# Attention and GEGLU on one core: unit transposes by DMA with the product on GpSimd, GELU bursts over two batches, and a planner that knows the port shared by VectorE and GpSimd

## The chip, the core and the metric

The kernel runs on one core of one Trainium2 chip. The engines are named as the profile names them: PE (TensorE, matrix products), ACT (ScalarE, here the softmax exp and GELU), DVE (VectorE), POOL (GpSimd), SP (the queue that issues DMAs). The kernel divides PSUM, into which PE writes, into eight banks of 128 x 512 fp32. Time runs some 2 us longer than the profiled span of the same run.

## The reference

One transformer block, 2048 tokens wide 640: 32 query heads of 20 that share one key and value head, then a GEGLU feed-forward layer of 1536.

```python
h  = x + attention(layernorm(x), wq, wk, wv, wo)
h2 = h + feed_forward(layernorm(h), w_gate, w_up, w_down)
# attention: scores = q k^T * 20**-0.5; p = softmax(scores); (p v) wo, no mask
# feed_forward: (gelu(x w_gate) * (x w_up)) w_down, tanh form of GELU
```

## The kernel before

The program is written by a small list scheduler that runs when the kernel is built. It keeps a clock for each engine, takes the engine that is free first, and commits the best ready operation with a cost in ns. The engines then run these lists in order, with semaphores. A wrong cost is no error in the result; it yields an order in which an engine later waits.

The work on scores is what fills the time. There are 512 packs of four score tiles (128 keys x 512 columns). PE computes a pack into four banks. Each tile goes either to ACT (a true exp) or to DVE (an exp made of one multiply-add whose integer result is read as bf16). A DVE tile needs two shifted copies as well, made by adding a constant ("shift-add"), mostly on POOL, and costs three products with v where an ACT tile costs one. The scheduler chooses 0, 1 or 2 tiles of a pack for DVE by how busy DVE is; while ACT is in a GELU burst it may give DVE all four.

Sixteen packs make a unit (32 units, two or four of them a "chunk" of tokens). A unit's sum leaves PSUM as `osb`, is transposed and divided by the softmax sum:

```python
def on_job(u, so):                      # before: transpose on PE by identity
    for j in range(4):
        pieces.append((mm(..., osb[:, so, j*P:(j+1)*P], ident[:], True, True), ...))
    # then, from PSUM: DVE reciprocal of the sums, and DVE products into onq (two per unit)
```

When all units of a chunk are done, wo, the second layernorm and the feed-forward layer of that "batch" (nine batches, 0 to 8) run under the exps of later chunks. The gate products are copied to `gbuf` by DVE; when a batch's are complete, ACT runs GELU over them in one burst and goes back to exp. After the last exp what is left runs as a tail, and there GELU is applied from PSUM directly.

```python
if gate_left[b] == 0:                   # before: one burst per batch
    gelu(b)                             # then: up products, then down products
```

When PE has been busy less than half of the last 3.4 us, the scheduler adds products with zeros ("fills").

The softmax here doesn't subtract the row's maximum and nothing guards it: scores larger than these inputs give would overflow.

## Time and profile before

804.31 us median of 3 runs (803.94 to 805.19). The profiled run was a further one of 806.45 us.

| engine | busy us | share of the 804.6 us span |
|---|---|---|
| ACT | 750.6 | 93% |
| PE | 693.7 | 86% |
| DVE | 627.2 | 78% |
| POOL | 586.2 | 73% |

The groups of instructions of the kernel before, shapes kept apart: engine, operation, output and inputs, shapes, count, busy us and mean ns of one, idle time before them and what ended it.

```profile
L1486 POOL TENSOR_TENSOR pd<-pd,shifts 128x512 int32<-128x512 int32 x517 | 534.8, 1043 | 170.5 <-DVE pd L1509 161.1 <-PE ps L510 4.8 <-DVE ln_veb L419 1.4
L1423 ACT ACTIVATE pa<-ps 128x1024 bf16<-128x1024 f32 x449 | 484.7, 1082 | 2.4 <-PE ps L1083 2.3
L1509 DVE TENSOR_SCALAR pd<-ps 128x512 uint16<-128x512 f32 x587 | 395.3, 687 | 142.3 <-PE ps L1083 131.3
L1423 ACT ACTIVATE pa<-ps 128x512 bf16<-128x512 f32 x563 | 354.9, 653 | 23.8 <-PE ps L1083 19.2
...
L472 DVE TENSOR_SCALAR xn_tmp<-xh,mv,ln_r 128x640 bf16<-128x640 bf16 x32 | 21.4, 686 | 0.4
L1466 DVE TENSOR_SCALAR pd<-pd 128x512 uint16<-128x512 uint16 x43 | 21.4, 502 | 0.0
...
L668 DVE TENSOR_TENSOR onq<-ps,rcp 128x160 bf16<-128x160 f32 x56 | 16.0, 317 | 0.7
...
L829 ACT ACT_TABLE_LOAD x7 | 9.0, 1283 | 0.1
L1423 ACT ACT_TABLE_LOAD x7 | 9.0, 1283 | 0.0
```

ACT ran 449 x 2 + 563 = 1461 exp tiles, DVE 587. The mean shift-add of 512 columns on DVE took 502 ns (276 at best) and the mean normalisation 686 (422 at best). Seven GELU bursts of one batch cost 7 + 7 table loads, and an eighth load to GELU follows in the tail.

Busy us of each engine in stretches of time, before; the columns after POOL are PE's granted clock, the share of the DMA engines and GB/s.

```profile
core 0: us, PE busy (x) PEld busy (x) DVE busy (x) ACT busy (x) POOL busy (x), PEclk, DMA share, GB/s
100.00:200.00 100.00, 85.77 (x1572) 38.98 (x1572) 81.42 (x145) 97.10 (x140) 77.37 (x81) 0.97 0.04 9
600.00:700.00 100.00, 90.59 (x1962) 44.43 (x1958) 77.81 (x137) 98.28 (x138) 76.07 (x76) 0.98 0.06 13
160.00:165.00 5.00, 1.68 (x24) 0.51 (x21) 4.98 (x9) 4.97 (x5) 3.34 (x4) 0.85 0.00 0
165.00:170.00 5.00, 4.75 (x60) 1.60 (x52) 1.88 (x5) 4.31 (x7) 0.95 (x1) 0.50 0.01 2
```

In the long stretches ACT is busy 97 to 98%: attention is bound by ACT.

The timeline of ACT before, near the end: start, length, instruction, count, idle time before it.

```profile
728.50 1.28 ACT L829 ACT_TABLE_LOAD   x1
729.79 2.86 ACT L829 ACTIVATE gbuf<-gbuf 128x1536 bf16<-128x1536 bf16 x2
732.66 1.28 ACT L1423 ACT_TABLE_LOAD   x1
733.95 2.49 ACT L1423 ACTIVATE pa<-ps 128x512 bf16<-128x512 f32 x4
...
770.51 8.34 ACT L1423 ACTIVATE pa<-ps 128x512 bf16<-128x512 f32 x12 [0.17 <-PE ps L1083]
778.87 1.28 ACT L811 ACT_TABLE_LOAD   x1
```

The burst is 1.28 + 2.86 + 1.28 us, back to back. The last exp ends at 770.51 + 8.34 = 778.9 us, so the tail is 804.6 - 778.9 = 25.7 us.

### The profile page before, as it was taken

The page shows a single profiled execution, that of the slowest core. Times are in us where ns is not written, and L with a number is a line of the kernel's source. Part 1 is how long each engine was busy: PE and PEld are TensorE (multiplying, and loading weights), DVE is VectorE, ACT ScalarE, POOL GpSimd, SP SyncE. Part 2 cuts the span into 40 slices and gives each one's busy share as a digit, 9 for nine tenths or more (in the row PEclk, how much of TensorE's full clock was granted, in tenths as well). Part 3 has the DMA queues.
Part 4 walks back from the last instruction along what each step waited for, and adds up shares of the span by engine and source line. Part 5 has one row for each costly group of instructions (what it writes and reads, how often), then busy time and mean ns, then how long its engine had stood idle before and what let it go on. Part 6 is the DMA issues. An engine that isn't in the chain of part 4 may idle for free.

```text
span 804.6 us, 29858 instructions
## 1 busy us (share of the span) xinstructions
PE 693.7 (86%) x13162; PEld 332.3 (41%) x13162; DVE 627.2 (78%) x1156; ACT 750.6 (93%) x1065; POOL 586.2 (73%) x624
## 2 busy tenths in 40 slices
PE   5687778989978998789988799888998899887998
PEld 3332223534434443345433444334444444343457
DVE  7868789877887778877788777988779776877864
ACT  5899999999989999899999999999999999999981
POOL 4587877868767677767878678877777668776760
PEclk9999999989999999999999999999999999998999
DMA  7680001000100000000000000000010000100000
GB/s 198 118 311 2 2 13 24 3 2 2 35 19 3 2 20 18 18 3 3 19 19 18 3 2 19 19 19 2 2 35 19 3 2 19 19 18 11 11 19 18
DMA packets 40288, 21.96 MB, mean 27 GB/s; under 512 B 31328, under 2 KB 38880, under 8 KB 40160
## 3 DMA queue, kind: packets, MB, share of 16 engines
q1 hardware_dynamic: 38848, 19.61, 9.6%
q8 instruction: 105, 1.72, 0.9%
q10 hardware_dynamic: 1312, 0.44, 0.3%
q14 instruction: 23, 0.19, 0.1%
HBM read 10.21 MB, written 2.62 MB: 16 GB/s over the span
## 4 chain that ended last, share of the span: by engine, by line
PE 46%; DVE 25%; ACT 25%; issue 2%; DMA 1%; POOL 1%; POOLq 0%; DVEq 0%
ACT pa L1423 25%; PE ps L510 17%; DVE pd L1509 15%; PE ps L1083 13%; PE ps L1162 13%; DVE pd L1466 3%; PE ps L506 3%; DVE xn_tmp L472 2%; DVE osb L1189 1%; DVE stats L403 1%; DVE qT L580 1%; DVE xh L728 1%; DVE onq L668 1%; DMA onT<-onq 1%; DVE ln_vb L415 0%
## 5 line engine op out<-in xcount | busy, mean ns | idle before, releaser
L1423 ACT ACTIVATE pa<-ps 128x512 bf16<-128x512 f32 (+1 forms) x1012 | 699.4, 844 | 26.2 <-PE ps L1083 21.5
L1486 POOL TENSOR_TENSOR pd<-pd,shifts 128x512 int32<-128x512 int32 x517 | 534.8, 1043 | 170.5 <-DVE pd L1509 161.1
L1509 DVE TENSOR_SCALAR pd<-ps 128x512 uint16<-128x512 f32 x587 | 395.3, 687 | 142.3 <-PE ps L1083 131.3
L1162 PE MATMUL ps<-pd,v_ext 128*32 128x512 bf16 x1761 | 276.2, 400 | 28.0 <-DVE osb L1189 21.5
L1162 PE MATMUL ps<-pa,v_ext 128*32 128x512 bf16 x1461 | 265.4, 393 | 2.7 <-ACT pa L1423 1.3
L1083 PE MATMUL ps<-qT,kT 32*128 32x512 bf16 x2048 | 206.8, 390 | 65.9 <-DVE pd L1509 41.0
L1083 PEld LDWEIGHTS ps<-qT,kT 32*128 32x128 bf16 x2048 | 58.9, 91 | 233.7 <-DVE pd L1509 161.3
L1162 PEld LDWEIGHTS ps<-pd,v_ext 128*32 128x32 bf16 x1761 | 74.8, 98 | 79.1 <-issue 35.0
L1162 PEld LDWEIGHTS ps<-pa,v_ext 128*32 128x32 bf16 x1461 | 70.6, 96 | 43.1 <-issue 30.3
L510 PE MATMUL ps<-xn2T,wg_sb 128*32 128x256 bf16 (+1 forms) x1720 | 66.1, 278 | 0.1
L510 PE MATMUL ps<-xn2T,wu_sb 128*32 128x256 bf16 x1680 | 64.9, 276 | 0.5 <-DVE onq L668 0.4
L510 PE MATMUL ps<-wd_sb,gbuf 128*32 128x320 bf16 x1344 | 64.4, 301 | 0.2 <-DVE onq L668 0.2
L510 PE MATMUL ps<-xn1T,wq_pad 128*32 128x256 bf16 (+1 forms) x1440 | 51.0, 267 | 0.2
L510 PEld LDWEIGHTS ps<-xn2T,wu_sb 128*32 128x32 bf16 x1680 | 42.9, 97 | 18.7 <-issue 10.3
L510 PEld LDWEIGHTS ps<-xn2T,wg_sb 128*32 128x32 bf16 x1720 | 42.1, 98 | 17.6 <-issue 11.5
L510 PEld LDWEIGHTS ps<-wd_sb,gbuf 128*32 128x32 bf16 x1344 | 33.5, 96 | 23.8 <-issue 11.8
L510 PEld LDWEIGHTS ps<-xn1T,wq_pad 128*32 128x32 bf16 x1440 | 33.8, 98 | 13.8 <-issue 8.9
L846 DVE TENSOR_TENSOR gbuf<-ps,gbuf 128x512 bf16<-128x512 f32 x48 | 32.9, 685 | 6.6 <-PE ps L506 6.4
L1466 DVE TENSOR_SCALAR pd<-pd 128x512 uint16<-128x512 uint16 (+2 forms) x66 | 37.8, 595 | 0.0
L1472 POOL TENSOR_TENSOR pd<-pd,shifts 128x256 int32<-128x256 int32 x48 | 30.2, 635 | 3.9 <-DVE pd L1509 3.4
L403 DVE BATCH_NORM_STATS2 stats<-xh 128x6 f32<-128x320 bf16 x64 | 29.9, 477 | 1.3 <-DMA xh<-in_A_x_dram 1.1
L809 DVE CAST gbuf<-ps 128x512 bf16<-128x512 f32 x42 | 28.7, 683 | 1.0 <-PE ps L510 0.9
(71 smaller groups left out, 357.8 us busy)
## 6 DMA issues: line engine op xcount, KB each, us to landing
out_dram<-xh SPq DMA_DIRECT2D x16, 160.0 KB, 1.8
xh<-in_A_x_dram SPq DMA_DIRECT2D x3, 640.0 KB, 6.3
wg_sb<-in_B_w_gate_dram SPq DMA_DIRECT2D x1, 1920.0 KB, 9.3
wu_sb<-in_B_w_up_dram SPq DMA_DIRECT2D x1, 1920.0 KB, 13.6
wd_sb<-in_B_w_down_dram SPq DMA_DIRECT2D x1, 1920.0 KB, 18.0
wo_sb<-in_A_wo_dram SPq DMA_DIRECT2D x1, 800.0 KB, 5.5
gbuf<-in_A_wq_dram ACTq DMA_DIRECT2D x1, 400.0 KB, 4.6
gbuf<-in_A_wq_dram SPq DMA_DIRECT2D x1, 400.0 KB, 6.9
```

What stands on the lines that cost most here:

```text
L403: dve(lambda e: e.bn_stats(stats[:, ln, t, 6 * h:6 * h + 6], xh[:, t, h * HALF:(h + 1) * HALF]), 395, [key], [("st", ln, t, h)], prio, c)
L506: return e.matmul(o(b), l, r, start=st, stop=sp)
L510: ins = e.matmul(o(b)[a, :], l[:, a], r, start=st, stop=sp, tile_position=(0, 32 * j))
L809: dve(lambda e: e.tensor_copy(o, i), c_dve(n * k), [("b", bk)], ks, 1.0, fin)
L846: dve(lambda e: e.tensor_tensor(o, i, o, ALU.mult), c_dve(n * k), [("b", bk)] + ks, ks, 1.0, fin)
L1083: ins = e.matmul(bank(b), kT4[32 * r:32 * r + 32, kt * P:(kt + 1) * P], qT[32 * r:32 * r + 32, s, :], start=True, stop=True, tile_position ...
L1162: ins = e.matmul(ps[32 * r:32 * r + 32, ab * 512:(ab + 1) * 512], v_ext[:, it["kt"], it["w"], :], it["ap"], start=st, stop=(j in ends), ti ...
L1423: op = plan.commit("act", lambda e: e.activation(dst, src, ACT.Exp, scale=SM_SCALE), cost, L_ACT, [("b", b0 + i) for i in range(n)], [("pa ...
L1466: return e.tensor_scalar(pd[:, w, a], pd[:, 0, a], float(CH_SHIFT[w]), None, ALU.add)
L1472: return e.tensor_tensor(pd32[:, w, h], pd32[:, 0, h], shifts[:, w - 1:w].to_broadcast([P, 256 * k]), ALU.add)
L1486: return e.tensor_tensor(pd32[:, 1:3, h], pd32[:, 0, h].unsqueeze(1).to_broadcast([P, 2, 256]), shifts[:].unsqueeze(2).to_broadcast([P, 2, ...
L1509: op = plan.commit("dve", lambda e: e.tensor_scalar(pd[:, 0, s * 512:(s + 1) * 512], bank(b), CH_A, CH_B, ALU.mult, ALU.add), c_dve(512), ...
```

## The change

The intent: take the unit transposes off PE and their product off DVE, halve the switches of ACT's table, let the planner know that some DVE operations and POOL exclude each other, and let score packs use spare PSUM banks more often. The diff, cut to its core:

```diff
+    MERGE = [(0, 1), (2, 3), (4, 5), (6, 7), (8,)]
+    PE_ON = (30, 31)            # the last two units stay on PE
+    POOL_NM = 750.0
-    POOL_ADD = 635.0            # planned ns of a shift-add on POOL: one copy
-    POOL_ADD2 = 1200.0          # both copies
+    POOL_ADD = 580.0
+    POOL_ADD2 = 1010.0
...  # planned ns of a normalisation
-            tk = _Task(("dve",), None, 420, L_DVE, ...)
+            tk = _Task(("dve",), None, 320, L_DVE, ...)
...  # unit transpose, units 0 to 29: DMA, DVE reciprocal from SBUF, product on POOL
+    tk.fn = lambda e: e.dma_start_transpose(onr[:, s, :]..., osb[:, so, :])
+    dve(fn, 400, ...) if key[0] == "b" else task(("pool",), fn, POOL_NM, ...)
...  # GELU only when all batches of a group have their gates
+    def gated(b):
+        grp = next(m for m in MERGE if b in m)
+        if all(gate_left[x] == 0 for x in grp):
+            for x in grp:
+                if copied[x]:
+                    gelu(x)
...  # port: a locking DVE operation (normalisation, shift-add) waits for POOL in the plan, and POOL for it
+        if lock:
+            for o in self.ops["pool"][-2:]:
+                if o.t0 <= t0 < o.end:
+                    t0 = o.end
+            self.port = t0 + cost
+        elif eng == "pool":
+            t0 = max(t0, self.port)
...
+            if tk.lock and plan.free["pool"] > t + LOCKW:      # LOCKW = 200
+                continue
+        if YIELD and ... plan.free["dve"] < t + YIELD:         # POOL holds back, YIELD = 700
...  # planned cost of a DVE shift-add of k*512 columns
-        k * 512 / 1.92 + 72.0
+        k * 512 / 3.84 + 72.0
...  # spare score banks
-        if not us or active or any(u["acc"] is None for u in us) or len(us) > 1: return False
-        if len(us[-1]["left"]) < 3: return False
-        return not state["misc_ready"]
+        if active or state["misc_ready"]: return False
+        if state["kv_left"] > 0 or not any(u["acc"] is not None for u in us): return False
+        return True                                            # SPK = 1
```

More of the change, by code (lines that the diff above doesn't have):

```diff
@@ L46, in __init__ @@
         self.free = {e: 0.0 for e in self.ENGINES}
+        self.port = 0.0
         self.w = {}
@@ L75, in ready, with commit @@
         return t
-    def commit(self, eng, fn, cost, lat, reads=(), writes=(), at=0.0, dma=False):
+    def commit(self, eng, fn, cost, lat, reads=(), writes=(), at=0.0, dma=False, lock=False):
         deps = self._deps(eng, reads, writes)
         t0 = max([self.free[eng], at] + [o.vis for o in deps])
+        if lock:
[5 more added lines that the diff above has]
+            t0 = max(t0, self.port)
         op = _Op(eng, fn, deps, t0, t0 + cost, t0 + cost + lat, dma)
@@ L162 @@
 class _Task:
-    __slots__ = ("engs", "fn", "cost", "lat", "reads", "writes", "prio", "then", "gate", "born")
+    __slots__ = ("engs", "fn", "cost", "lat", "reads", "writes", "prio", "then", "gate", "born", "lock")
     def __init__(self, engs, fn, cost, lat, reads, writes, prio, then=None, gate=None):
@@ L176, in __init__ @@
         self.gate = gate
+        self.lock = False
 class _Job:
@@ L263, in bass_sequential_preLN__grouped_kv_mqa__glu_gated_geglu__prompt_kernel @@
     osb = sb("osb", [P, 2, 512], BF16)
+    onr = sb("onr", [P, 2, 512], BF16)
     rcp = sb("rcp", [P, 2, 16], F32)
@@ L333, in bass_sequential_preLN__grouped_kv_mqa__glu_gated_geglu__prompt_kernel @@
     NP0 = 4
+    LNT = 12
+    SPK = 1
+    LOCKW = 200.0
+    YIELD = 700.0
     WQA = 1
@@ L378, in bass_sequential_preLN__grouped_kv_mqa__glu_gated_geglu__prompt_kernel @@
     bank_owner = {b: None for b in range(8)}
-    slots = {"xt": list(range(NXT)), "q": list(range(NQ)), "onT": list(range(4)), "osb": [0, 1], "rcp": [0, 1]}
+    slots = {"xt": list(range(NXT)), "q": list(range(NQ)), "onT": list(range(4)), "osb": [0, 1], "rcp": [0, 1], "onr": [0, 1]}
     pa_free = [True] * NA
@@ L467, in norm @@
             keys = [("x", t)] if ln == 0 else [("h", t, 0), ("h", t, 1)]
-            tk = _Task(("dve",), None, 420, L_DVE, keys + [("lr", kk)], [], prio, then, gate)
+            tk = _Task(("dve",), None, 320, L_DVE, keys + [("lr", kk)], [], prio, then, gate)
+            tk.lock = True
             def bind():
@@ L624, in q_job, with normed @@
         jobs.append(jb)
-    def on_job(u, so):
+    def normed(u, so, v, key, done):
         tl, gs = u["tiles"], u["groups"]
         nt, G = len(tl), len(gs)
-        pieces = []
-        for j in range(4):
-            pieces.append((mm((lambda j: lambda b: ps[:, b * 512 + j * P:b * 512 + (j + 1) * P])(j),
-                              osb[:, so, j * P:(j + 1) * P], ident[:], True, True), c_mm(128),
-                           [("osb", so), "ident"]))
-        def then(b):
-            slots["osb"].append(so)
-            sr = slots["rcp"].pop(0)
-            v5 = bank(b).rearrange("p (j r e) -> p j r e", j=4, r=4)
-            def c1(op):
-                cnt = [0]
-                parts = []
-                rv = rcp[:, sr, :].rearrange("p (j r) -> p j r", j=4)
-                if nt == 4:
-                    g = gs[0]
-                    o = onq[:, onslot[tl[0]]:onslot[tl[0]] + 4, 4 * Dh * g:4 * Dh * (g + 1)].rearrange(
-                        "p j (r d) -> p j r d", r=4)
-                    parts.append((o, slice(0, 4)))
-                elif nt == 2:
-                    for gi, g in enumerate(gs):
-                        o = onq[:, onslot[tl[0]]:onslot[tl[0]] + 2, 4 * Dh * g:4 * Dh * (g + 1)].rearrange(
-                            "p j (r d) -> p j r d", r=4)
-                        parts.append((o, slice(2 * gi, 2 * gi + 2)))
-                else:
-                    o = onq[:, onslot[tl[0]], 4 * Dh * gs[0]:4 * Dh * (gs[-1] + 1)].rearrange(
-                        "p (j r d) -> p j r d", j=4, r=4)
-                    parts.append((o, slice(0, 4)))
-                def c2(op):
-                    cnt[0] += 1
-                    if cnt[0] == len(parts):
-                        free_bank(b)
-                        slots["rcp"].append(sr)
-                        unit_normed(u)
-                for o, js in parts:
-                    nj = js.stop - js.start
-                    dve((lambda o, js, nj: lambda e: e.tensor_tensor(
-                        o, v5[:, js, :, 0:Dh], rv[:, js, :].unsqueeze(3).to_broadcast([P, nj, 4, Dh]), ALU.mult))(
-                            o, js, nj), c_dve(80 * nj), [("b", b), ("rcp", sr)],
-                        [("onq", onslot[t], g) for t in tl for g in (gs if nj == 4 else [gs[js.start // 2]])],
-                        0.9, c2)
-            dve(lambda e: e.reciprocal(rcp[:, sr, :].rearrange("p (j r) -> p j r", j=4), v5[:, :, :, Dh]), 200,
-                [("b", b)], [("rcp", sr)], 0.8, c1)
@@ L677, in gate, with bind, c1, c2 @@
+        v4 = v.rearrange("p (j r e) -> p j r e", j=4, r=4)
         def gate():
             return bool(slots["rcp"]) and all(x in on_sent for t in tl for x in on_before[t])
-        jobs.append(_Job(("on", u["id"]), 1.5, pieces, then, gate))
+        sl = []
+        def bind():
+            sr = slots["rcp"].pop(0)
+            sl.append(sr)
+            tk.writes = [("rcp", sr)]
+            tk.fn = lambda e: e.reciprocal(rcp[:, sr, :].rearrange("p (j r) -> p j r", j=4), v4[:, :, :, Dh])
+        def c1(op):
+            sr = sl[0]
+            o = onq[:, onslot[tl[0]]:onslot[tl[0]] + nt, 4 * Dh * gs[0]:4 * Dh * (gs[-1] + 1)]
+            o = o.rearrange("p t (g r d) -> p g t r d", g=G, r=4)
+            i0 = v4[:, :, :, 0:Dh].rearrange("p (g t) r d -> p g t r d", g=G)
+            i1 = rcp[:, sr, :].rearrange("p (g t r) -> p g t r", g=G, t=nt).unsqueeze(4).to_broadcast(
+                [P, G, nt, 4, Dh])
+            def c2(op):
+                slots["rcp"].append(sr)
+                done()
+                unit_normed(u)
+            fn = (lambda e: e.tensor_tensor(o, i0, i1, ALU.mult))
+            ks = [("onq", onslot[t], g) for t in tl for g in gs]
+            if key[0] == "b":
+                dve(fn, 400, [key, ("rcp", sr)], ks, 0.9, c2)
+            else:
+                task(("pool",), fn, POOL_NM, L_POOL, [key, ("rcp", sr)], ks, 0.9, c2)
@@ new lines, in normed, with on_job, then, bind @@
+        tk = _Task(("dve",), None, 120, L_DVE, [key], [], 0.8, c1, gate)
+        tk.born = bind
+        tasks.append(tk)
+    def on_job(u, so):
+        if u["id"] in PE_ON:
+            pieces = []
+            for j in range(4):
+                pieces.append((mm((lambda j: lambda b: ps[:, b * 512 + j * P:b * 512 + (j + 1) * P])(j),
+                                  osb[:, so, j * P:(j + 1) * P], ident[:], True, True), c_mm(128),
+                               [("osb", so), "ident"]))
+            def then(b):
+                slots["osb"].append(so)
+                normed(u, so, bank(b), ("b", b), lambda: free_bank(b))
+            jobs.append(_Job(("on", u["id"]), 1.5, pieces, then,
+                             lambda: all(x in on_sent for t in u["tiles"] for x in on_before[t])))
+            return
+        tk = _Task(("sp",), None, 1330, 1500, [("osb", so)], [], 0.5, None, lambda: bool(slots["onr"]))
+        sl = []
+        def bind():
+            s = slots["onr"].pop(0)
+            sl.append(s)
+            tk.writes = [("onr", s)]
+            tk.fn = lambda e: e.dma_start_transpose(onr[:, s, :].rearrange("p (j i) -> p j i", j=4), osb[:, so, :])
+        def sent(op):
+            s = sl[0]
+            slots["osb"].append(so)
+            normed(u, so, onr[:, s, :], ("onr", s), lambda: slots["onr"].append(s))
+        tk.born = bind
+        tk.then = sent
+        sp_tasks.append(tk)
@@ L726, in fin @@
                 free_bank(b)
-                ln_half(1, t, h, 4.0 if t < 12 else 0.7, ln2_after[t])
+                ln_half(1, t, h, 4.0 if t < LNT else 0.7, ln2_after[t])
             dve(lambda e: e.tensor_tensor(xh[:, t, h * HALF:(h + 1) * HALF], xh[:, t, h * HALF:(h + 1) * HALF],
@@ L797, in fin @@
                 copied[b].append(fc)
-                if gate_left[b] == 0:
-                    gelu(b)
+                gated(b)
             def fin2(op):
@@ L804, in fin2 @@
                 up_job(b, fc)
-                if gate_left[b] == 0 and copied[b]:
-                    gelu(b)
+                gated(b)
             o, i = gview(b, fc, k), bview(bk, b, k)
@@ L885, in bass_sequential_preLN__grouped_kv_mqa__glu_gated_geglu__prompt_kernel @@
     for gl in LN2G:
-        aft = ln_group(1, gl, 4.0 if gl[0] < 12 else 0.7, x2_done)
+        aft = ln_group(1, gl, 4.0 if gl[0] < LNT else 0.7, x2_done)
         for t in gl:
@@ L970, in spare_ok @@
     def spare_ok():
+        if active or state["misc_ready"]:
+            return False
         us = open_units()
-        if not us or active or any(u["acc"] is None for u in us) or len(us) > 1:
-            return False
-        if len(us[-1]["left"]) < 3:
-            return False
-        return not state["misc_ready"]
+        if SPK == 0:
+            return bool(us) and len(us) == 1 and us[0]["acc"] is not None and len(us[-1]["left"]) >= 3
+        if state["kv_left"] > 0 or not any(u["acc"] is not None for u in us):
+            return False
+        return SPK == 1 or len(us[-1]["left"]) != 16
     def free_banks(t):
@@ L1382, in run_task @@
                 cost += 1283.0
-        op = plan.commit(eng, tk.fn, cost, lat, tk.reads, tk.writes, at=t)
+        op = plan.commit(eng, tk.fn, cost, lat, tk.reads, tk.writes, at=t, lock=tk.lock)
         if tk.then:
@@ L1462, in do_adds @@
         a = slice(s0 * 512, (s0 + k) * 512)
-        cost, lat = (k * 512 / (1.92 if POOL_ADD else 3.84) + 72.0, L_DVE) if eng == "dve" else (POOL_ADD, L_POOL)
+        cost, lat = (k * 512 / 3.84 + 72.0, L_DVE) if eng == "dve" else (POOL_ADD, L_POOL)
         if eng == "dve":
@@ L1473, in fn @@
                                        shifts[:, w - 1:w].to_broadcast([P, 256 * k]), ALU.add)
-        op = plan.commit(eng, fn, cost, lat, [("pd", 0, s0 + i) for i in range(k)] + [("sh", w)], [("pd", w, s0 + i) for i in range(k)], at=t)
+        op = plan.commit(eng, fn, cost, lat, [("pd", 0, s0 + i) for i in range(k)] + [("sh", w)], [("pd", w, s0 + i) for i in range(k)], at=t, lock=eng == "dve")
         for x in recs:
@@ L1574, in pool_decide @@
     def pool_decide(t):
+        if YIELD and state["kv_left"] == 0 and plan.free["dve"] < t + YIELD:
+            for tk in tasks:
+                if tk.lock and known(tk) and (tk.gate is None or tk.gate()) and plan.ready(
+                        "dve", tk.reads, tk.writes) <= t + YIELD:
+                    return False
         best = None
```

## The prediction

> **What bounds it now.** The page gives a span of 804.6 us with ScalarE busy 750.6 us (93%), PE 693.7 (86%), DVE 627.2 (78%), POOL 586.2 (73%). The busy table by windows shows ScalarE at 96 to 99% of every 100 us stretch from 100 to 700 us, the others at 74 to 91%. After the last softmax exp (779 us, timeline) a serial tail of 26 us runs. The scheduler shares out 2048 score tiles: by the groups ScalarE did 1461 (699.4 us, 0.479 us each), DVE 587 (687 ns each, then shift-adds, mostly on POOL at 1043 ns).
>
> **What the change does.**
> 1. GELU bursts over two batches. ScalarE loads a table 15 times besides the first, 1.283 us each (groups). The Trainium skill ("ScalarE: Activation LUTs", What ACT_TABLE_LOAD costs) adds a drain of about 1.38 us per switch; this trace shows none (timeline at 728.5 us: 1.28 load, 2.86 GELU, 1.28 load, back to back). Pairing leaves 7 to 9 loads: 8 to 10 us less, on the critical path.
> 2. For 30 of 32 units the identity transpose leaves PE (496 matmuls, 16 us) for a DMA transpose (today's land in 2.7 us), and the product leaves DVE (18 us) for POOL. POOL's adds (256 elements 635 ns, 512 elements 1043 ns) give an estimate of 740 ns for 320 elements: 22 us on POOL, which has 218 us idle.
> 3. Ordering against the port that DVE and POOL share. "SBUF — State Buffer", SBUF: two separate sides, calls the pair an exclusive lock held for a whole instruction. The trace agrees: DVE's shift-add takes 276 ns at best, 502 on average for 512 elements; the normalisation 422 and 686. Avoiding this is worth at most 24 us of DVE; I count 12 to 15.
> 4. Spare score banks are allowed more often, also between units (the waits show PE stopped some 20 times for the accumulator's eviction, up to 3.5 us). This trims ScalarE's 22 us of waits for scores.
>
> **Critical path.** PE, DVE and POOL savings do not count by themselves. The 30 us of DVE relief pay only as score tiles move from ScalarE to DVE: I expect 20 to 40 tiles, each 0.479 us: about 14 us. With 9 us of table loads and 3 us of fewer bubbles the exps end near 753 us.
> Against it: pairing batches 6 and 7 holds batch 6's GELU, up and down products until tile 14's gates are done. Before, they ran at 728 to 777 us, under the exps; part will land in the tail, which I expect to grow from 26 to 31 us.
>
> **Predicted time: 784 us, range 769 to 798** (before 804.3). Chances: faster by over 2% 0.66, within 2% 0.31, slower by over 2% 0.03.
>
> **What would show each step.** Table loads fall to 7 to 9. Exps on ScalarE below 1450, on DVE above 600. PE's ident products nearly gone; the product on POOL at about 0.75 us x30. Mean DVE shift-add and normalisation nearer 300 and 450 ns. POOL busy 610 to 650 us. Last exp near 753 us, tail 29 to 34 us.
>
> **What would make it wrong.** The planner spends DVE's relief on shift-adds taken back from POOL, so ScalarE's count stays and only table loads pay (792 to 796). In-order queues: a late DMA transpose stalls DVE or POOL and with them the score tiles. Longer bursts starve PE. Or PE (86%) becomes the bound, as each tile moved costs two further PV products.

## More of the kernel before

The metric is device time in microseconds (us).

The page of the kernel before: busy time, share and instruction count of each engine, and the clock granted to PE in 40 slices of the span, in tenths.

```profile
PE 693.7 (86%) x13162; PEld 332.3 (41%) x13162; DVE 627.2 (78%) x1156; ACT 750.6 (93%) x1065; POOL 586.2 (73%) x624
...
PEclk9999999989999999999999999999999999998999
```

## The result

791.55 us median of 6 runs (789.72 to 793.77) against 805.01 of 6 runs of before. The ratio is 0.9835 (95% interval 0.9814 to 0.9856): 1.65% faster. Ratios are the mean time of one kernel's runs over that of the other's of the same rounds, so not quite the ratio of the medians quoted. The predicted 784 us lay 7.6 us lower; the measured time is inside the range, and the class is "within 2%", to which I gave 0.31.

The page of the changed kernel, the same two lines:

```profile
PE 688.1 (87%) x12613; PEld 327.8 (42%) x12613; DVE 622.6 (79%) x1128; ACT 728.2 (92%) x1054; POOL 626.9 (80%) x683
...
PEclk9799999999999999999999999999999999999999
```

Groups of the changed kernel:

```profile
L1529 POOL TENSOR_TENSOR pd<-pd,shifts 128x512 int32<-128x512 int32 x531 | 544.8, 1041 | 94.6 <-DVE pd L1552 88.5 <-DVE ln_vb L433 1.7 <-DVE ln_veb L437 1.4
L1466 ACT ACTIVATE pa<-ps 128x1024 bf16<-128x1024 f32 x427 | 461.9, 1084 | 3.8 <-PE ps L1126 2.7 <-PE ps L1205 1.0
L1552 DVE TENSOR_SCALAR pd<-ps 128x512 uint16<-128x512 f32 x608 | 408.4, 688 | 127.9 <-PE ps L1126 117.1
L1466 ACT ACTIVATE pa<-ps 128x512 bf16<-128x512 f32 x586 | 365.3, 655 | 17.3 <-PE ps L1126 13.0
...
L1509 DVE TENSOR_SCALAR pd<-pd 128x512 uint16<-128x512 uint16 x51 | 25.0, 492 | 0.0
L674 POOL TENSOR_TENSOR onq<-onr,rcp 128x320 bf16<-128x320 bf16 x30 | 22.1, 736 | 9.5 <-DVE rcp L660 9.4
...
L491 DVE TENSOR_SCALAR xn_tmp<-xh,mv,ln_r 128x640 bf16<-128x640 bf16 x32 | 19.4, 613 | 0.3
...
L870 ACT ACT_TABLE_LOAD x3 | 3.8, 1283 | 0.1
L1466 ACT ACT_TABLE_LOAD x3 | 3.8, 1283 | 0.0
```

ACT now runs 427 x 2 + 586 = 1440 exp tiles, DVE 608. Table loads besides the first fell from 15 to 7 (3 + 3, and one in the tail). The product stands on POOL, 30 x 736 ns. But the mean shift-add and normalisation on DVE are 492 and 613 ns: hardly shorter.

ACT's timeline, changed kernel, near the end, and after it the busy table by windows (columns as before).

```profile
735.35 15.22 ACT L1466 ACTIVATE pa<-ps 128x512 bf16<-128x512 f32 x22 [0.46 <-PE ps L1126]
750.59 1.28 ACT L845 ACT_TABLE_LOAD   x1
...
753.42 3.37 ACT L870 ACTIVATE gbuf<-gbuf 128x1536 bf16<-128x1536 bf16 x3
763.86 0.70 ACT L598 ACTIVATE xn2T<-ps 128x640 bf16<-128x640 bf16 x1 [7.08 <-PE ps L539]
772.62 0.60 ACT L845 ACTIVATE gbuf<-ps 128x512 bf16<-128x512 f32 x1 [8.05 <-PE ps L525]
```

```profile
600.00:700.00 100.00, 92.90 (x1930) 45.73 (x1926) 78.33 (x132) 97.98 (x137) 80.81 (x83) 1.00 0.11 18
250.00:255.00 5.00, 4.22 (x84) 1.94 (x76) 4.91 (x9) 4.97 (x5) 4.41 (x5) 1.00 0.00 0
255.00:260.00 5.00, 3.79 (x75) 2.04 (x79) 4.69 (x9) 4.98 (x6) 4.66 (x6) 1.00 0.01 3
750.00:788.00 38.00, 34.68 (x404) 28.73 (x395) 16.48 (x33) 8.80 (x11) 1.20 (x2) 1.00 0.05 19
```

The last exp ends at 735.35 + 15.22 = 750.6 us, 28.3 us earlier than before. The tail is 787.5 - 750.6 = 36.9 us, 11.2 us longer. 28.3 - 11.2 = 17.1 us is the whole difference of the two spans. The medians differ by 13.5 us only: the profile before is of a run (806.45 us) slower than all six of the result, the profile of the changed kernel is of its fastest run (789.72). Some 3.6 us of the accounts below are therefore the choice of runs. The tail is bound by PE, busy 34.68 of the 38 us in the last row; from the last exp on PE's busy time rose from 22.8 to 34.1 us, as much as the tail. The burst at 251 us, twice as long as one before, did not starve PE: 4.22 and 3.79 of 5 us, clock 1.00.

The 28.3 us before the last exp divide as follows: 8 table loads fewer, 10.3 us; the exps' busy time from 699.4 to 689.0 (the page's group of both shapes), 10.4 us; two of the GELU instructions of 1475 ns moved past the last exp, 3 us; the remaining 4.6 us is nearly all less idle time on ACT (34.5 us before the last exp, 30.6 in the changed kernel). Its waits for scores, the first line for each kernel in the table of waits (total us, times, longest), fell by 5.7 us. First before, then changed:

```profile
ACT pa L1423 <- PE ps L1083: 21.5, 46, 1.5
```

```profile
ACT pa L1466 <- PE ps L1126: 15.8, 32, 1.6
```

What the tail gained is seen in the groups of products that PE runs with full 128-column weights, as it does only once no attention work is left. Before, then changed:

```profile
L506 PE MATMUL ps<-wd_sb,gbuf 128*128 128x320 bf16 x48 | 7.0, 299 | 0.0
```

```profile
L525 PE MATMUL ps<-wd_sb,gbuf 128*128 128x320 bf16 x96 | 13.5, 299 | 0.0
...
L525 PE MATMUL ps<-xn2T,wu_sb 128*128 128x256 bf16 x60 | 6.9, 272 | 0.0
```

Another 48 down products and 60 up products of 256 columns are in the tail, 6.5 + 6.9 us of PE: the feed-forward work of batch 6, done under the exps before. (The kernel before has no up products of 256 columns in this form.)

### The profile page after: what moved, and what is told of

The parts are those of the page before. It is cut to its first block, busy times and chain, and to the rows that moved or that the text cites. A ratio compares the mean times of both kernels' runs of the same rounds, so it can differ in the third digit from the quotient of the medians.

```text
span 787.5 us, 28823 instructions
## 1 busy us (share of the span) xinstructions
PE 688.1 (87%) x12613; PEld 327.8 (42%) x12613; DVE 622.6 (79%) x1128; ACT 728.2 (92%) x1054; POOL 626.9 (80%) x683
## 4 chain that ended last, share of the span: by engine, by line
PE 49%; ACT 30%; DVE 15%; DMA 2%; issue 2%; POOL 2%; POOLq 0%
ACT pa L1466 28%; PE ps L529 18%; PE ps L1126 13%; PE ps L1205 13%; DVE pd L1552 9%; PE ps L525 4%; ACT gbuf L870 1%; DVE xn_tmp L491 1%; DVE osb L1232 1%; DMA onr<-osb 1%; POOL pd L1529 1%; DMA xn1T<-xn_tmp 1%; DVE pd L1509 1%; DMA onT<-onq 1%; DVE gbuf L887 1%
## 5 line engine op out<-in xcount | busy, mean ns | idle before, releaser
L1466 ACT ACTIVATE pa<-ps 128x1024 bf16<-128x1024 f32 (+1 forms) x1013 | 689.0, 836 | 21.1 <-PE ps L1126 15.8
L1529 POOL TENSOR_TENSOR pd<-pd,shifts 128x512 int32<-128x512 int32 x531 | 544.8, 1041 | 94.6 <-DVE pd L1552 88.5
L1552 DVE TENSOR_SCALAR pd<-ps 128x512 uint16<-128x512 f32 x608 | 408.4, 688 | 127.9 <-PE ps L1126 117.1
L1205 PE MATMUL ps<-pa,v_ext 128*32 128x512 bf16 x1440 | 256.7, 385 | 3.1 <-ACT pa L1466 2.5
L1205 PEld LDWEIGHTS ps<-pa,v_ext 128*32 128x32 bf16 x1440 | 68.3, 95 | 39.2 <-issue 24.2
L529 PE MATMUL ps<-wd_sb,gbuf 128*32 128x320 bf16 x1152 | 57.7, 301 | 1.0 <-DVE gbuf L887 1.0
L529 PE MATMUL ps<-xn2T,wu_sb 128*32 128x256 bf16 x1440 | 58.1, 274 | 0.3 <-DVE gbuf L887 0.3
L529 PEld LDWEIGHTS ps<-xn2T,wu_sb 128*32 128x32 bf16 x1440 | 36.8, 96 | 16.3 <-issue 7.9
L1515 POOL TENSOR_TENSOR pd<-pd,shifts 128x256 int32<-128x256 int32 x63 | 41.6, 669 | 1.3 <-DVE pd L1552 1.3
L529 PEld LDWEIGHTS ps<-xn1T,wq_pad 128*32 128x32 bf16 x1440 | 34.5, 99 | 16.0 <-issue 8.4
L1509 DVE TENSOR_SCALAR pd<-pd 128x512 uint16<-128x512 uint16 (+1 forms) x70 | 36.5, 534 | 0.0
L529 PE MATMUL ps<-wo_sb,onT 128*32 128x320 bf16 x600 | 28.9, 301 | 1.3 <-DMA onT<-onq 0.7
```

Of the source, the lines that this page charges most:

```text
L529: ins = e.matmul(o(b)[a, :], l[:, a], r, start=st, stop=sp, tile_position=(0, 32 * j))
L1205: ins = e.matmul(ps[32 * r:32 * r + 32, ab * 512:(ab + 1) * 512], v_ext[:, it["kt"], it["w"], :], it["ap"], start=st, stop=(j in ends), ti ...
L1466: op = plan.commit("act", lambda e: e.activation(dst, src, ACT.Exp, scale=SM_SCALE), cost, L_ACT, [("b", b0 + i) for i in range(n)], [("pa ...
L1509: return e.tensor_scalar(pd[:, w, a], pd[:, 0, a], float(CH_SHIFT[w]), None, ALU.add)
L1515: return e.tensor_tensor(pd32[:, w, h], pd32[:, 0, h], shifts[:, w - 1:w].to_broadcast([P, 256 * k]), ALU.add)
L1529: return e.tensor_tensor(pd32[:, 1:3, h], pd32[:, 0, h].unsqueeze(1).to_broadcast([P, 2, 256]), shifts[:].unsqueeze(2).to_broadcast([P, 2, ...
```

## The experiments

All twelve runs gave correct results. Each is an edit of one part of the changed kernel, or of the kernel before where it says "alone"; e9 and e11 carry e3's 755 ns as well. "Loads" are table loads besides the first; "last exp" and "tail" are from the profiled run.

| run | median us | ratio to before, 95% interval | clock, median of runs | loads | DVE tiles | last exp | tail |
|---|---|---|---|---|---|---|---|
| before | 805 to 806.6 | 1 | 0.970 to 0.972 | 15 | 587 | 778.9 | 25.7 |
| changed | 791.6 | 0.9835 (0.9814 to 0.9856) | 0.989 | 7 | 608 | 750.6 | 36.9 |
| e1 single bursts | 793.4 | 0.9833 (0.9805 to 0.9862) | 0.985 | 15 | 602 | 768.5 | 26.1 |
| e2 PE transposes | 801.4 | 0.9937 (0.9914 to 0.9960) | 0.990 | 7 | 598 | 761.3 | 37.7 |
| e3 neutral | 798.7 | 0.9910 (0.9883 to 0.9937) | 0.984 | 9 | 594 | 767.7 | 31.3 |
| e4 last pair split | 795.8 | 0.9868 (0.9845 to 0.9890) | 0.987 | 9 | 613 | 756.8 | 37.1 |
| e5 early pairs | 787.5 | 0.9773 (0.9749 to 0.9797) | 0.989 | 11 | 608 | 758.9 | 26.4 |
| e6 no port order | 808.4 | 1.0034 (1.0012 to 1.0055) | 0.985 | 7 | 625 | 769.6 | 35.8 |
| e7 bursts alone | 799.6 | 0.9934 (0.9902 to 0.9965) | 0.991 | 7 | 579 | 760.8 | 37.3 |
| e8 DMA alone | 801.8 | 0.9951 (0.9929 to 0.9973) | 0.987 | 15 | 599 | 773.7 | 27.1 |
| e9 as e6, 755 ns | 809.3 | 1.0052 (1.0026 to 1.0078) | 0.981 | 7 | 620 | 770.4 | 35.8 |
| e10 no order, old costs | 799.0 | 0.9925 (0.9909 to 0.9942) | 0.990 | 7 | 612 | 757.7 | 38.4 |
| e11 as e5, 755 ns | 794.5 | 0.9889 (0.9853 to 0.9925) | 0.987 | 11 | 597 | 764.1 | 28.0 |
| e12 old spare rule | 799.1 | 0.9938 (0.9905 to 0.9971) | 0.983 | 7 | 575 | 760.4 | 35.8 |

### e3: the yardstick

```diff
-    POOL_NM = 750.0
+    POOL_NM = 755.0
```

> A yardstick: the planner is told 755 instead of 750 ns for the GpSimd product, nothing else. Nothing about the work changes, only the order that the planner finds. If schedule luck is small, within 1 us of 791.5. If it is large, 3 to 6 us away, most likely slower (the planner's own end is 4.4 us later); then no single run of another variant can be read closer than that.

It was 0.75 points slower than the changed kernel. The program does the same work in another order, so by itself the order found can be worth nearly half of the whole gain. (2.6 us can be seen: one exp fell behind the burst of batches 6 and 7, which cost two more table loads.) This is the most useful run: an edit that reshuffles the order from early on can owe 0.75 points to the order alone. One such pair gives a size and no upper limit, so single differences of 0.5 to 1.0 points below are not read as the worth of a part. A verdict then has to rest on something that the trace shows directly (the count of loads, the place of the last exp, the length of the tail), or on two pairs.

### e1: bursts of one batch again

```diff
-    MERGE = [(0, 1), (2, 3), (4, 5), (6, 7), (8,)]
+    MERGE = [(b,) for b in range(9)]
```

> The changed kernel with every GELU burst of one batch again (15 table loads besides the first instead of 7). Theory A (the bursts give back in the tail what they save): exps end about 10 us later than the 750.6 us of the changed kernel, near 761, but the tail after the last exp falls from 37 to about 27 us, so the time stays within 4 us of 791.5. Theory B (the bursts are the gain, as table loads sit on the critical path): about 800 us or more, tail unchanged near 37 us.

The ratio is that of the changed kernel, 0.9833 against 0.9835. ACT's timeline of this run:

```profile
731.51 37.01 ACT L1466 ACTIVATE pa<-ps 128x512 bf16<-128x512 f32 x54
768.54 1.28 ACT L845 ACT_TABLE_LOAD   x1
```

The exps end at 768.5, not 750.6, and the tail is 26.1 us, not 36.9. Theory A holds in direction in both halves: with the rest of the change in place, the pairs save time on ACT and give it back in the tail. The exps came 18 us later, not 10; 10.3 of that is table loads and 3 us GELU work back under the exps. The profiled run was also the slowest of the four (796.72 us at a clock of 0.974; the median is 793.4), which may account for some 3 us; the rest I cannot separate from the order.

### e4: which pair makes the tail long

```diff
-    MERGE = [(0, 1), (2, 3), (4, 5), (6, 7), (8,)]
+    MERGE = [(0, 1), (2, 3), (4, 5), (6,), (7,), (8,)]
```

> The changed kernel with only the last pair of batches (6 and 7) split; the order is the same until about 700 us. Theory T1 (batch 6's held-back products alone lengthen the tail): tail falls from 37 to about 27 us, exps end 4 to 6 us later, time about 786. Rival T2 (all the pairs together push the feed-forward work later, so that it is too late for batch 6 whatever the last pair does): tail stays 35 to 38 us and the time is 790 to 796.

The tail stayed at 37.1 us and the time was 795.8 us. The prediction had blamed the pair 6-7 alone, and that fell. ACT's timeline:

```profile
741.59 1.28 ACT L870 ACT_TABLE_LOAD   x1
...
747.04 9.79 ACT L1466 ACTIVATE pa<-ps 128x512 bf16<-128x512 f32 x15
```

Batch 6 has its burst, but at 741.6 us, only 15 us before the last exp. Before, that burst stood at 728.5 us, 50 us before it; in e1 at 726.1, 42 us before it. The earlier pairs hold the whole feed-forward chain back: batch 4 waits for batch 5's gates, and batch 6 needs the columns of `gbuf` that batch 4 gives free. The groups of this run agree: all 96 down products of batches 6 to 8 are in the tail, as in the changed kernel, and 31 of the 60 up products of batch 6.

### e5 and e11: pairs early only

```diff
-    MERGE = [(0, 1), (2, 3), (4, 5), (6, 7), (8,)]
+    MERGE = [(0, 1), (2, 3), (4,), (5,), (6,), (7,), (8,)]
```

> The changed kernel with batches 0-1 and 2-3 paired and all later ones single (11 table loads besides the first). Theory (pairs cost only through the late feed-forward work): half of the table loads are still saved (about 5 us) and the tail is short again, 27 to 29 us against 37, so about 786 us. Rival (a burst's saving is always given back or is schedule luck): 790 to 797.

787.5 us, ratio 0.9773, better than both kernels; its interval is clear of that of the changed kernel. The 0.62 points are less than the neutral run moved, but this edit reshuffles less: in the traces the order of instructions on DVE and POOL is that of the changed kernel until 547 us (e3 leaves it at 112 us), and the DVE tiles (608) and ACT's waits for scores (15.9 against 15.8 us) are the same. ACT's timeline:

```profile
718.90 1.28 ACT L870 ACT_TABLE_LOAD   x1
...
724.35 34.56 ACT L1466 ACTIVATE pa<-ps 128x512 bf16<-128x512 f32 x50
758.92 1.28 ACT L845 ACT_TABLE_LOAD   x1
```

Batch 6's burst is at 718.9 us again, 40 us ahead of the last exp at 758.9, and the tail is 785.3 - 758.9 = 26.4 us with 11 loads in place of 15. Against the changed kernel the last exp came 8.3 us later, of which four more loads are 5.1 us and the two GELU instructions of batch 6 are 2.9, and the tail is 10.5 us shorter.

The same edit with 755 ns told for the product, to be set against e3:

> Early pairs only, at the second planner seed, to be set against the neutral run at 755 (0.991 of before). If early pairs are better by the shorter tail and not by luck: tail 27 to 32 us and a ratio to before below 0.991; the planner's own end is 1.8 us earlier than that of its partner, so I expect 0.985 to 0.991.

Ratio 0.9889 against e3's 0.9910, the tail 28.0 against 31.3 us: the same direction, but the intervals overlap. (In e3 the burst of batches 6 and 7 happened to fall just ahead of the last exp, so its tail was shorter than the changed kernel's.) e11 and e3 likewise have one order until 552 us. That early pairs keep the tail short is shown in both runs; that they are worth 0.6 points for every order is not.

### e6, e9, e10: the port ordering

```diff
-            tk.lock = True
+            tk.lock = False
...
-        ..., at=t, lock=eng == "dve")
+        ..., at=t, lock=False)
-    YIELD = 700.0
+    YIELD = 0.0
```

> The changed kernel with the ordering against the shared port taken out (no operation is marked as locking, GpSimd never holds back); costs as changed. If the ordering is worth what the prediction counted: mean DVE shift-add and normalisation return to about 500 and 690 ns, DVE gets 12 to 15 us more busy time, time 795 to 801. Rival (it was hardly worth anything, as the durations after the change barely fell): within 3 us of 791.5, durations within 10% of those of the changed kernel.

808.4 us, slower than the kernel before. Neither expectation named the right mechanism in full: the means on DVE rose only to 536 ns (shift-add of 512) and 651 ns (normalisation), and DVE even took 625 tiles. The loss is on ACT, which waited twice as long for scores as in the changed kernel. The wait line of ACT, and the timeline at 108 us:

```profile
ACT pa L1466 <- PE ps L1126: 32.2, 67, 1.8
```

```profile
108.16 1.36 DVE L1509 TENSOR_SCALAR pd<-pd 128x512 uint16<-128x512 uint16 x2
...
109.44 1.96 DVE L1552 TENSOR_SCALAR pd<-ps 128x512 uint16<-128x512 f32 x3
...
109.57 0.39 PE L1205 MATMUL ps<-pa,v_ext 128*32 128x512 bf16 x2 [0.46 <-DVE pd L1509]
...
110.02 3.18 ACT L1466 ACTIVATE pa<-ps 128x512 bf16<-128x512 f32 x5 [0.47 <-PE ps L1205]
```

Two DVE shift-adds, planned at 512 / 3.84 + 72 = 205 ns each, took 1.36 us while POOL's shift-adds ran from 107.29 to 111.4 us without a break; that POOL's hold on the port is the reason is inferred from this overlap. PE's next products with v waited 0.46 us for the shift-adds (109.57), and ACT sat idle 0.47 us until those products released its exps at 110.02. The three DVE score tiles behind the shift-adds started only at 109.44. This is one case followed through; ACT's other waits, most of them for the scores line itself, were counted and not each traced to a shift-add. Between 40 and 200 us ACT was busy 142.5 of 160 us in this run and 156.1 in the changed kernel; between 200 and 740 us 521.2 and 527.6 of 540. In the first stretch the profiled run also had a lower granted clock (0.94 against 1.00). It was low from 40 to 60 and from 150 to 170 us only; in the other 120 us, at 1.00 in both runs, ACT still lost 6.2 of the 13.6 us, as it lost 6.4 from 200 to 740 us, also at 1.00. So at least 12.6 of the 20.1 us have another cause than the clock at the time.

The same with 755 ns, against e3:

> The run without port ordering at a second planner seed (755 ns told for the GpSimd product), to be set against the neutral run at 755, which was 0.991 of before. If the loss of the first such run (2.0% against the changed kernel) is the missing order: again clearly slower than its partner, 803 us or more. If it was schedule luck: 794 to 802, on either side of its partner.

Ratio 1.0052 against 0.9910, ACT's waits for scores 31.8 us against 18.3. Two pairs, 2.0 and 1.4 points, beyond the yardstick: with these costs the ordering is needed.

With the old, padded costs of the shift-adds as well. (The expectation calls this the whole ordering part; the planned normalisation stays at the new 320 ns, where the kernel before had 420.)

```diff
-    POOL_ADD = 580.0
-    POOL_ADD2 = 1010.0
+    POOL_ADD = 635.0
+    POOL_ADD2 = 1200.0
...
-        k * 512 / 3.84 + 72.0
+        k * 512 / (1.92 if POOL_ADD else 3.84) + 72.0
```

> The changed kernel without the port ordering and with the planner's old, padded durations (GpSimd add of both copies 1200 ns and of one 635, DVE shift-add at half speed): the whole ordering part undone. Theory P (what counts is that the plan leaves room for the collisions, in whichever way): the padding does most of the job, 792 to 800 us. Rival O (the order itself, which keeps them from colliding, is what counts): 804 us or more, as without order alone.

Ratio 0.9925, close to the yardstick and 1.1 points better than e6, with which it shares the missing order. This speaks for theory P: what counts is that the plan leaves room for the collision. The kernel before did so by padding, the changed one by modelling the port. Trimmed costs without the model are the worst of the three. It is one run; ACT's waits for scores were 24.2 us, between the 15.8 of the changed kernel and the 32.2 of e6. What the model is worth against padding, I cannot tell from the luck of the order.

### e2, e8: the transposes

```diff
-    PE_ON = (30, 31)
+    PE_ON = tuple(range(32))
```

> The changed kernel with all 32 unit transposes back on PE, and the product back on DVE as one instruction. Theory A (the gain is in the relief of DVE and PE): about 10 us slower, near 801, with fewer exps on DVE or more ScalarE waits. Theory B (the bursts are the gain): within 3 us of 791.5.

Ratio 0.9937: slower than the changed kernel by 1.0 points, with DVE tiles down from 608 to 598 and the last exp at 761.3. By the letter theory A was met; but the neutral run, in which only the order moved, lost 0.75 points and 14 DVE tiles, so this run cannot settle it.

The opposite edit, DMA transposes and the POOL product on the kernel before and nothing else (`on_job` and `normed` of the changed kernel in place of the old `on_job`, with `onr`, `PE_ON`, `POOL_NM`):

> The kernel before with only the 30 transposes by DMA and the product on GpSimd. Theory (this is the main gain): 795 to 799, DVE exps up by 10 or more from 587. Rival (the relief needs the port ordering or the spare banks to be turned into moved tiles): 803 to 808, DVE exps within 5 of 587.

Ratio 0.9951 (801.8 us), between the two expectations, though DVE tiles did rise from 587 to 599. That is the direction predicted, but the neutral run moved 14 tiles by order alone, so neither the 12 tiles nor the 0.5 per cent is shown to be the worth of the transposes.

### e7: bursts alone

The kernel before with `MERGE` and `gated` of the changed kernel, in place of the two calls of `gelu(b)`.

> The kernel before with only the GELU pairs. Theory (bursts give back in the tail what they save): exps end some 6 to 10 us before 779, tail 36 to 39 instead of 26 us, time 803 to 812. Rival (bursts are a gain by themselves): about 796.

799.6 us: faster than my theory said. The last exp was at 760.8 (18 us earlier) and the tail 37.3 (11.6 longer), so it was given back only in part. The order, which is another one here too, or the clock, next, may be what I had not counted.

### e12: the spare banks

```diff
-    SPK = 1
+    SPK = 0
```

> The changed kernel with the old rule for spare score banks. The prediction counted some 3 us for the new rule. If so: 793 to 798 us, ScalarE's waits for scores up from 16 us, DVE exps down. If the spare banks are worth nothing: within the schedule luck on both sides, 789 to 793. If they are a larger part of the gain: 800 or more.

Ratio 0.9938, slower by 1.0 points. ACT's waits for scores were 16.4 us, not above the changed kernel's 15.8, so that part of the expectation failed. DVE tiles fell from 608 to 575, the largest fall of all edits of the changed kernel and more than the neutral run's 14. The scheduler weighs the free banks when it chooses whether DVE gets a second tile, so the rule seems to work through the share of tiles rather than through bubbles; no second pair was run. Its worth in time is not told from the order.

### The granted clock

The kernel before was granted a mean PE clock of 0.966 to 0.981 in 22 runs, the changed kernel 0.987 to 0.991 in its six. Cut into windows of 10 us from 40 to 770 us, the trace before has 12 windows with a clock under 0.97, that of the changed kernel none; of the 12, those at 160, 260, 350, 360, 450, 640 and 730 us hold a GELU burst or follow one within 10 us; the other five (80, 230, 240, 330, 710) do not. Within one kernel the clock and the time go together: in one set of seven runs of before, five at 0.970 took 805.9 to 806.9 us and two at 0.977 took 803.8 and 804.0. A straight line through the deviations of 75 runs from the means of their own kernel and round has a slope of -3.3 us for 0.01 of clock (standard error 0.4). From 0.971 to 0.989 that is about 6 us: an estimate, by correlation alone, of 6 of the 13 us gained. It would also explain e7: at 0.991 against 0.970 the same line gives some 7 us, about all that it gained. No run held the order fixed and set the clock, so this is argued and not shown. A rival stands: whatever makes PE wait can both lengthen a run and lower its clock, without the one causing the other. Nor does the clock rank the kernels: e2 and e10 have 0.990 and took 801.4 and 799.0 us. Which part of the change keeps PE from starving in the bursts is open: e7 and e8 each raised the clock.

## Why the prediction was right or wrong

The range and the direction held. The gain was 13 us where 20 were predicted, and the class that was given 0.66, over 2% faster, did not come. A miss of 7.6 us is hardly more than what the order alone moved in e3 (some 6 us by the ratios), so how close the number came is partly luck. Point by point:

1. *Table loads 7 to 9, 8 to 10 us off the critical path.* Right: 7, and 10.3 us, without a drain.
2. *Transposes and product.* Right in form and size: 30 products on POOL at 736 ns (estimated 740), POOL busy 626.9 (predicted 610 to 650).
3. *Less collision on the port, 12 to 15 us of DVE.* Wrong. Shift-adds and normalisations together took 59.2 us before (37.8 + 21.4) and 56.6 after (37.2 + 19.4): about 3 us. "Nearer 300 and 450 ns" was 492 and 613. e6, e9 and e10 show what stands in its place: ordering, and by one run padding, keeps a collision from surprising the plan, and the price of a surprise is ACT's idle time (32.2 us of waits for scores against 15.8) far more than DVE's busy time.
4. *Tiles moved, 20 to 40.* Right at the low end: 21, though in the neutral order only 7. The exps' busy time fell by 10.4 us where 14 was predicted.
5. *Spare banks, 3 us of bubbles.* ACT's waits for scores fell by 5.7 us; but in e12 these waits hardly changed (16.4) and the share of tiles did, so the fall is not shown to come from the banks.
6. *Last exp near 753 us.* The number was right, 750.6, partly by luck: the DVE relief behind it was too large, and in its place stand 3 us of GELU work that moved past the last exp, less idle time on ACT and a profiled run that was the fastest.
7. *"The tail, which I expect to grow from 26 to 31 us".* This is the failed term: 36.9 us. 753 + 31 was the sum; 750.6 + 36.9 = 787.5 came out, 3.5 us more. The other 4 us of the miss are the 2.2 us between span and time and the 1.8 us by which the profiled run lay under the median. The mechanism was named (batch 6's products fall past the last exp) but only "part" of them was counted; all of its down and up products went there, 13.4 us of PE in a tail that is bound by PE. And it was put down to the last pair alone, while e4 shows that the earlier pairs cause it too.

The prediction's worry that PE would become the bound was met in the tail, not in attention. It feared that longer bursts starve PE; in the profile of the changed kernel they did not. It missed that PE was starved in the bursts before, with a clock of 0.50 after it, and that an order may be worth 6 us by luck.

Shown, then, are the loads saved, the tail that they cost (e1, e4, e5 and e11) and the loss without port order at trimmed costs (two pairs). How the rest of the 13 us divides among the transposes, the spare banks, the clock and the order is open: no run stands far enough out of the yardstick.

## What to carry to other kernels

Batching table switches on a bound engine delays whatever waits for the batch; look where that work lands before counting the saving, and batch only where there is time left to catch up (early pairs here, not late ones). In a kernel whose order comes from a planner, run neutral changes first (better several than the one here): an ablation that moves the time no more than they do shows nothing by its time. An edit that leaves most of the order as it was can be read closer. Here a planned cost that was too short on a shared resource was worse than a padded one (1.0034 against 0.9925), and the engine that paid was the bound one, waiting for its input.

## What the Trainium skill lacked or had wrong

- "ScalarE: Activation LUTs", What ACT_TABLE_LOAD costs: it gives 1283 ns for the load, which this trace shows exactly, and about 1380 ns of drain for every switch, which it does not show. The exp before ends at 728.5 us, GELU starts at 729.79 and the next exp at 733.95, 1.30 us after the GELU ended at 732.65.
- "SBUF — State Buffer", SBUF: two separate sides: the exclusive lock agrees (in e6 two DVE shift-adds of 512 columns took 1.36 us while POOL was busy without a break; before, one took 276 ns at best). It says nothing of the cost downstream: without room in the plan ACT's waits for scores went from 15.8 to 32.2 us.
- "TensorE: Matmul & The Clock Gate", Part 1: The HAM clock gate, says that about 3.4 us of idleness halves the clock. The trace before agrees in the half, after a stretch that was not wholly idle: from 160.7 to 164.4 us PE ran only four score products (at 162.54), and from 164.43 its products of 512 columns took some 0.61 us instead of 0.39, with a clock of 0.50 from 165 to 170 us. Not on the page: what it costs a kernel bound by another engine, here some 3.3 us of 800 go with 0.01 of mean clock, an estimate by correlation.
- "GPSIMD Engine Reference", 3.1, has as its measured two-tensor operation an fp32 add of 2048 columns. Not there: a bf16 by fp32 product of 320 columns with a broadcast operand takes 736 ns, an int32 add of 512 columns 1041 ns.
- "DMA: Bandwidth & Descriptors", DMA Transpose (X-bar): no time for a small transpose within SBUF. Here 128 x 512 bf16 landed 2.4 us after issue (median of 30, longest 4.3).
